# Attention scores on two row halves of the array in fp16 words, the softmax in place in PSUM, and its result turned by transfers

## The chip, the cores and the metric

The kernel runs on one core of a Trainium2 chip. The metric is device time in microseconds (us) of one execution; lower is better. PE is the TensorE matrix engine (PEld its weight loads), DVE the VectorE, ACT the ScalarE, POOL the GpSimd engine, SP the queue that issues the transfers (DMA).

## The reference, cut to what matters

Eight sequences (B) of 576 positions (S), eight heads (H) of 64 dimensions (D). Attention with a decay comes first, then a feed-forward block of 1024 channels on 4608 tokens of 512 features.

```
scores = (q @ k.T) / sqrt(D)                        # per b, h: 576 x 576
cum    = cumsum(log(clip(f, 1e-4, 1)))
scores = where(causal, -1e9, scores + cum[i] - cum[j])
attn   = exp(scores - max); attn /= sum(attn) + 1e-9
x      = attn @ v                                   # heads side by side: 4608 x 512
h      = x @ w_in                                   # 4608 x 1024
solu   = h * softmax(h)
ln     = (solu - mean) / sqrt(var + 1e-6) * g_ln
out    = ln @ w_out                                 # 4608 x 512
```

## The kernel before, in words

Two heads form a pair; there are 32 pairs, four to a sequence. A pair's 576 queries are cut into five tiles, i = 0 to 4: one of 64 rows and four of 128. Tile i meets 64 + 128 i keys, so the five tiles have 64, 192, 320, 448 and 576 columns for each head. The first three tiles are "half 0" of a pair (320 queries), the other two "half 1" (256 queries). The feed-forward block runs in 36 layers of 128 tokens; four and a half layers use one sequence.

A number that has to be exact beyond fp16 is held as two words, high and low, and a product of two such numbers is three matmuls (high by high, low by high, high by low).

- **Loading.** `load` brings a pair's q and k into `raw`; `split_qk` cuts them into a high part `hi` (POOL) and a remainder left in `raw` (`parts`, DVE or POOL), in fp32r. The remainders and copies are then laid one under the other by many small transfers into `qs`, `ks`, `kz` and `qz`, so that one matmul contracts over 128 rows: 64 rows of the one part and 64 of the other. The decay `cum` stands in two more rows of `kz`.
- **Scores.** `score_products` (lines 657, 658): for each tile and head two fp32r matmuls into one of two PSUM banks `ps`. The four pairs of the first sequence do their half 0 in plain fp32 instead (`native`, line 655), so that the first layer can start early.
- **Softmax.** `scores`: DVE adds the causal mask, scales, writes the tile to `p` in SBUF and keeps the greatest value `nm` (line 678); ACT takes the exponent in place and its sum (681); DVE makes the inverse `ri` (692, 693); POOL multiplies `p` by it (708).
- **P turned.** `transposes`: PE turns `p` in pieces of 128 by 128 against `ident` (739) into two PSUM banks `ps_t`; ACT takes out the high word `pth` (333) and DVE the low word `ptl` (747). The widest tile, i = 4, goes another way from the fifth pair on: POOL (703) and DVE (705) make its two fp16 words `p16` in SBUF, and two transposing transfers (342) turn them.
- **Values.** `values`: P turned times v into a PSUM bank `ps_o`. The first block of keys is one product over both heads (778, "whole" array); the others are one product for each head on a half of the array's columns (782). ACT and DVE take out the words `x_h` and `x_l` (801, 802).
- **Layer.** `layer`: 24 matmuls of 512 columns into `hps` (818 to 820), the softmax and the norm on DVE, ACT and POOL (831 to 864), the result turned (by transfers in layers 5 to 29, by PE otherwise) into `zz`, and 24 matmuls of 512 columns into `ps_o` (888 to 890).

What stands where in each engine's queue is not written by hand: `Plan.schedule` replays the whole program with a cost for every operation and takes, on each engine, the ready operation with the smallest due time. The due times come from the tables `DUE`, `EARLY`, `AT_P`, `AT_L` and others. PSUM banks are handed out by pools: two banks for scores (`s`), two for turning (`t`), two for outputs (`o`); `hps` holds the last two of eight. Matmuls without use (line 991) fill the gaps that the plan sees on PE in its first 140 us.

Of the kernel before, what the change touches and what calls it, by code (L numbers as in the profile page):

```python
# [24 lines left out]
HALF_S = 320  # L25
MASK = -8.0e9
# [28 lines left out]
SWITCH = ((0.0, 40.0, 0.0, 95.0), (0.0, 0.0, 0.0, 95.0), (0.0, 10.0, 0.0, 95.0), (130.0, 230.0, 180.0, 0.0))  # L55
# [11 lines left out]
class Plan:  # L67
# [31 lines left out]
    def schedule(self):  # L99
# [11 lines left out]
        for _ in self.ops:  # L111
            for e in stale:
# [78 lines left out]
DUE = dict(load=77.279, split=-5.82, upper=-59.07, v=-11.029, S=((-16.591, 2.389), (-10.866, -1.366), (-5.374, -8.943), (-5.783, 2.152), (-2.369, 2.528)), T=((-4.114,), (-6.578,), (0.027, -77.756), (12.862, 14.095), (-144.678, 29.668, 76.368)), V=((16.423, 371.464), (24.511, 165.955)))  # L191
EARLY = dict(load=-5.393, split=100.725, upper=-110.557, v=36.25, S=((216.478, -198.746), (23.491, -109.734), (23.153, -123.713), (-123.145, 60.456), (26.752, 113.365)), T=((-12.366,), (-36.759,), (-81.739, -143.07), (38.749, -11.206), (-229.138, -88.73, -36.262)), V=((-26.507, -137.733), (60.804, 84.836)))
PAIR = 23.079
C_OUT = 31.47
START = 86.666
HALF = ((64.967, -14.868), (32.745, -34.71))
W_IN = (-57.941, 54.591)
W_OUT = (103.025, 310.791)
LOAD = (198.891, -63.738)
WI_SCALE = (-43.671, -130.632)  # L200
VDUE = ((-38.21, -22.856, 38.942), (79.121, -21.859, -165.431), (55.69, -110.294, -55.795))
W_SCALE = 138.576
W_DMA = (-134.941, 217.289)
LAYER = PAIR * NPAIR / 4.5
AT_P = (-81.617, 13.065, -70.797, 41.914, 10.593, 20.603, -9.689, -6.751, -9.556, -4.733, 6.888, -145.035, -0.228, -5.232, -11.649, -239.734, 11.35, 1.454, -1.658, -3.713, -18.063, -464.917, -48.735, -17.963, -2.737, -28.57, 0.178, -5.187, -1.852, -244.035, -23.722, -77.279)
# [7 lines left out]
def tile_kernel(ctx: ExitStack, tc: tile.TileContext, qk, v, f, w_in, w_out, g_ln, out):  # L213

    nc = tc.nc  # L220
# [7 lines left out]
    plan = Plan(s=2, t=2, o=2)  # L228
# [22 lines left out]

    qz = [sb(f"qz_{c}", 2, w, dtype=F32R) for c, w in enumerate((320, 256))]
    pt = [sb("p_0", P)] + [sb(f"p_{i}", (2 * i + 1) * P) for i in range(1, NQ)]
    mask = sb("mask", S + P, dtype=BF16)

    def masks():
# [5 lines left out]
        nc.gpsimd.memset(pt[0], 0.0)  # L262
# [775 lines left out]
```

## Time and profile before

| | |
|---|---|
| time, three runs | 761.96, 762.23 (median), 763.01 us |
| span of the profiled execution | 757.0 us; 5.2 us less than the median run |
| PE busy | 722.8 us (95% of the span), 4983 matmuls, 462 of them fillers |
| DVE, ACT, POOL busy | 608.3 us (80%), 474.1 us (63%), 456.7 us (60%) |
| transfers | 133.87 MB, 75.3% of sixteen DMA engines' span |
| TensorE clock granted | 0.998 on average |

A time in the text is in us from the start of the span. A matmul's busy time includes the pipeline behind it, so two matmuls that follow each other at once overlap in such a row; what a matmul costs PE is read from the distance between starts. A row "x24" counts 24 instructions.

### The profile page before, as it was taken

How to read it: one execution, taken by the hardware profiler on the slowest of the kernel's cores; microseconds unless marked ns; L12 is line 12 of the kernel's file. 1: busy time of each engine (PE TensorE's matmuls, PEld its weight loads, DVE VectorE, ACT ScalarE, POOL GpSimd, SP SyncE). 2: the span in 40 equal slices, each digit the busy share in tenths (PEclk: the TensorE clock that was granted, in tenths of full speed). 3: DMA queues.
4: the chain of work that ended last, by engine and by line, in shares of the span. 5: the costliest groups of instructions: out<-in, count | busy, mean ns of one | idle time of the engine just before them, and what ended most of it. 6: DMA issues, size and time to landing. Idle time of an engine off the chain costs nothing. (4 is left out here: it accounts for less than half of the span.)

```text
span 757.0 us, 15810 instructions
## 1 busy us (share of the span) xinstructions
PE 722.8 (95%) x4983; PEld 453.5 (60%) x4983; DVE 608.3 (80%) x1828; ACT 474.1 (63%) x1239; POOL 456.7 (60%) x645
## 2 busy tenths in 40 slices
PE   8998999988999999999999999999999999999998
PEld 7775676655656566555556666555565555554445
DVE  6557888899997899989599999999897869883343
ACT  5698977676665667755466677655565556653333
POOL 5537496656674787668377777775786666531220
PEclk9999999999999999999999999999999999999999
DMA  9557948968879898989789899889899788442001
GB/s 320 139 210 207 272 115 223 206 169 213 197 172 214 173 239 177 225 207 213 165 188 211 200 228 213 202 206 192 189 206 202 146 192 166 95 106 42 29 15 42
DMA packets 176851, 134.87 MB, mean 178 GB/s; under 512 B 128704, under 2 KB 139712, under 8 KB 175744
## 3 DMA queue, kind: packets, MB, share of 16 engines
q1 hardware_dynamic: 176768, 133.87, 75.3%
q8 instruction: 39, 0.64, 0.4%
q14 instruction: 44, 0.36, 0.2%
HBM read 39.51 MB, written 10.03 MB: 65 GB/s over the span
## 5 line engine op out<-in xcount | busy, mean ns | idle before, releaser
L681 ACT ACTIVATE p<-p,nm 128x320 f32<-128x320 f32 (+4 forms) x320 | 177.1, 554 | 88.7 <-DVE nm L678 83.4
L708 POOL TENSOR_SCALAR p<-p,ri 128x192 f32<-128x192 f32 (+4 forms) x264 | 153.2, 594 | 90.2 <-DVE ri L693 66.2
L678 DVE CUSTOM_DVE_ANT_0 p<-ps,mask 128x320 f32<-128x320 f32 (+4 forms) x320 | 126.3, 419 | 16.0 <-PE ps L658 11.2
L657 PE MATMUL ps<-ks_f32r,qs_f32r 128*128 128x448 f32 (+4 forms) x360 | 120.6, 359 | 4.6 <-DVE nm L678 3.7
L333 ACT ACTIVATE pth_f<-ps_t 128x512 f16<-128x512 f32 (+4 forms) x200 | 85.2, 442 | 46.1 <-PE ps_t L739 41.3
L818 PE MATMUL hps<-wi_h,x_h 128*128 128x512 f16 x288 | 109.9, 381 | 0.5 <-DVE e L840 0.5
L888 PE MATMUL ps_o<-wo_f,zz 128*128 128x512 f16 x280 | 106.8, 381 | 2.6 <-DMA zz<-z 2.2
L820 PE MATMUL hps<-wi_h,x_l 128*128 128x512 f16 x288 | 109.1, 379 | 0.0
L819 PE MATMUL hps<-wi_l,x_h 128*128 128x512 f16 x288 | 109.1, 379 | 0.0
L890 PE MATMUL ps_o<-wo_f,zz 128*128 128x512 f16 x280 | 106.1, 379 | 0.4 <-DVE zz L880 0.4
L889 PE MATMUL ps_o<-wo_f,zz 128*128 128x512 f16 x280 | 106.1, 379 | 0.0
L739 PE MATMUL ps_t<-ident,p 128*128 128x128 f32 x548 | 90.8, 279 | 13.1 <-DVE ptl_f L747 4.6
L658 PE MATMUL ps<-kz_f32r,qz 128*128 128x448 f32 (+4 forms) x360 | 100.8, 296 | 2.0 <-DMA kz_f32r<-c_scratch 1.2
L747 DVE TENSOR_TENSOR ptl_f<-ps_t,pth_f 128x512 f16<-128x512 f32 (+3 forms) x188 | 91.9, 502 | 8.1 <-ACT pth_f L333 7.7
L739 PEld LDWEIGHTS ps_t<-ident,p 128*128 128x128 f32 x548 | 64.4, 141 | 45.6 <-POOL p L708 13.0
L657 PEld LDWEIGHTS ps<-ks_f32r,qs_f32r 128*128 128x128 f32 (+1 forms) x360 | 64.9, 182 | 23.9 <-DVE nm L678 11.8
L589 POOL TENSOR_SCALAR hi<-raw 128x576 fp32r<-128x576 f32 (+1 forms) x64 | 48.4, 756 | 35.4 <-DMA kz_f32r<-raw 13.1
L658 PEld LDWEIGHTS ps<-kz_f32r,qz 128*128 128x128 f32 (+1 forms) x360 | 65.2, 182 | 5.1 <-issue 1.5
L850 POOL TENSOR_SCALAR st<-st 128x1 f32<-128x1 f32 x36 | 11.1, 308 | 89.0 <-ACT z L846 79.2
L703 POOL TENSOR_SCALAR wo_p<-p,ri 128x576 f16<-128x576 f32 x56 | 47.1, 851 | 27.9 <-DVE ri L693 14.8
L831 DVE TENSOR_REDUCE st<-hps 128x1 f32<-128x1024 f32 x36 | 43.9, 1218 | 21.1 <-PE hps L820 20.8
L681 ACT ACTIVATION_READ_ACCUMULATOR p<-p,nm 128x1 f32 (+1 forms) x320 | 60.1, 188 | 0.0
(194 smaller groups left out, 1416.2 us busy)
## 6 DMA issues: line engine op xcount, KB each, us to landing
raw<-in_qk_dram SPq DMA_DIRECT2D x32, 576.0 KB
ks_f32r<-hi SPq DMA_DIRECT2D x128, 144.0 KB
kz_f32r<-raw SPq DMA_DIRECT2D x64, 144.0 KB
vraw<-in_v_dram SPq DMA_DIRECT2D x28, 320.0 KB
out_dram<-y SPq DMA_DIRECT2D x35, 256.0 KB
qs_f32r<-hi SPq DMA_DIRECT2D x56, 144.0 KB
qs_f32r<-raw SPq DMA_DIRECT2D x56, 144.0 KB
qz<-hi SPq DMA_DIRECT2D x56, 80.0 KB
```

Of the source, the lines that this page charges most:

```text
L657: nc.tensor.matmul(dst, qs(p)[:, h, q0:q0 + nq], ks(p)[:, h, cols], start=True, stop=False)
L658: nc.tensor.matmul(dst, z[:, h, z0:z0 + nq], kz(p)[:, h, cols], start=False, stop=True)
L678: op(DVE, R_NS[i], at + 0.5, lambda a=a, e=e, key=key, o0=o0: nc.vector.tensor_tensor_reduce(pr[:, a:e], ps[plan.place[key]][:nq, o0:o0 + ...
L681: op(ACT, E_NS[i], at + 1.3, lambda: nc.scalar.activation(pr, pr, AF.Exp, bias=x, scale=-1.0, accum_out=sm[m][i][:nq, h:h + 1]), [("nm", m ...
L708: op(POOL, N_NS[j], at + 2.8, lambda g=g, j=j, pg=pg, r1=r1: nc.gpsimd.tensor_scalar(pg, pg, r1, 1.0, ALU.mult, ALU.mult), [("ri", m, j)], ...
L739: nc.tensor.transpose(tp[:, s, :], pt[i][:, k * P:(k + 1) * P], ident)
L818: nc.tensor.matmul(hps[:, sl], x_h, wi_h[:, c, sl], start=(c == 0), stop=False)
L819: nc.tensor.matmul(hps[:, sl], x_h, wi_l[:, c, sl], start=False, stop=False)
L820: nc.tensor.matmul(hps[:, sl], x_l, wi_h[:, c, sl], start=False, stop=(c == NCC - 1))
L888: nc.tensor.matmul(o, zz[a][:, 0, j], wo(0, k), start=(k == 0), stop=False)
L889: nc.tensor.matmul(o, zz[a][:, 0, j], wo(1, k), start=False, stop=False)
L890: nc.tensor.matmul(o, zz[a][:, 1, j], wo(0, k), start=False, stop=(k == NFC - 1))
```

## The change

Most of the attention is written anew, with new tables for the order. The layer's arithmetic stays.

- **q and k** become fp16 words, high and low, on the 64 rows of their own head: the two heads of a pair stand on rows 0 to 63 and 64 to 127 of one tile `qk16` and nothing is moved by transfers. So that fp16 holds them, q, k and v are scaled by powers of two per sequence: ACT sums their squares (`squares`, line 486) and `scale` works out three factors where it worked out one. High words are made on POOL (`Q_HI`), low words on DVE (567). The decay rows are now three bf16 words in `crow`.
- **Scores.** For a tile, each head has four matmuls on its half of the array's rows: three of words (606) and one that adds the decay rows (604); the two heads' matmuls alternate. Each head has a bank of its own. The plain fp32 start is gone.
- **Softmax in place.** Tiles 0 to 3 stay in their PSUM bank (`HOME`): mask, exponent, and both words of P are made from there, the high word on ACT (333), the low word on DVE (658). Tile 4 still goes through SBUF (`p_4`) and POOL. The bank comes free after the low word.
- **P turned** by transfers alone, for all tiles and pairs, both words in one transfer per tile.
- **Values** go tile by tile of queries: products of 64 or 128 columns (680, 683) where they had 128 to 320.
- **PSUM**: one pool of six banks, each a tile of its own, for scores, outputs and turning.
- **Layer**: `e`, `z` and `y` have two buffers; z is turned by transfers in layers 3 to 32, its high word is made by ACT and its low word by POOL (it was POOL and DVE). The last sequence's two halves are planned apart.

```
-P_32, X_32 = (1, 1, 2, 1), (1, 2, 2, 1, 1, 2, 1, 2)
-TURN = (450.0, 15.0, 1700.0)
+TURN = (1100.0, 22.0, 1700.0, 6.0)
-TURNED = (5, 30)
-Z_ENG = (3, 3, 1, 2)
+TURNED = (3, 33)
+Z_ENG = (3, 1)
+Z_LO = (3,) * 36
+Q_HI = (3,) * 32
+P_HI = (1, 1, 1, 1, 3)
+HOME = (1, 1, 1, 1, 0)
...
-    plan = Plan(s=2, t=2, o=2)
+    plan = Plan(s=NS)
...
-    ps = [pp.tile([P, 512], F32, name=f"ps{n}") for n in range(2)]
+    ps = [pp.tile([P, 512], F32, name=f"ps{n}") for n in range(NS)]
     hps = pp.tile([P, DFF], F32, name="hps")
-    ps_t = [pp.tile([P, 4, P], F32, name=f"ps_t{n}") for n in range(2)]
-    ps_o = [pp.tile([P, 512], F32, name=f"ps_o{n}") for n in range(2)]
...
-                    nc.tensor.matmul(dst, qs(p)[:, h, q0:q0 + nq], ks(p)[:, h, cols], start=True, stop=False)
-                    nc.tensor.matmul(dst, z[:, h, z0:z0 + nq], kz(p)[:, h, cols], start=False, stop=True)
+                for n, (x, y) in enumerate(((hi, hi), (lo, hi), (hi, lo), (None, None))):
+                    for h in range(2):
+                        k0 = P * (4 - i) if h == 0 else 0
+                        dst, cols = bank(p, i, h, int(a > 0))[:, :e - a], slice(k0 + a, k0 + e)
+                        if x is None:
+                            nc.tensor.matmul(dst, pattern[row(h)], crow[row(h), (p // NPAIR) % 2, p % NPAIR, cols], start=False, stop=True)
+                        else:
+                            nc.tensor.matmul(dst, x[row(h), 0, q0:q0 + P], y[row(h), 1, cols], start=(n == 0), stop=False)
...
+        def home(i, h, nq=P):
+            w = 64 + P * i
+            return bank(p, i, h)[:nq, :w] if HOME[i] else pt[i][:nq, h * w:(h + 1) * w]
...
-                op(POOL, N_NS[j], at + 2.8, lambda g=g, j=j, pg=pg, r1=r1: nc.gpsimd.tensor_scalar(
-                    pg, pg, r1, 1.0, ALU.mult, ALU.mult), [("ri", m, j)], [("p", j, g)])
+            copied(P_HI[j], {POOL: N_NS[j], ACT: 158 + 0.83 * w, DVE: 67 + 1.05 * w}, at[j][g] + STEPS[3], h16, lambda j=j, g=g, nq=nq: home(j, g, nq),
+                   reads, [("p16", n2, j, g)], scale=r1, clear=prior, port=not HOME[j])
...
-                nc.tensor.transpose(tp[:, s, :], pt[i][:, k * P:(k + 1) * P], ident)
+        turned_dma(at, lambda: turned_p(p, i).rearrange("p x s w -> p (x s) w"), lambda: p16(p, i)[:nq], nq // 16 * 2 * (2 * i + 1),
+                   [(x, m, i, h) for x in ("p16", "p16l") for h in range(2)], [("pt", m * (i < 3), i)], clear=to)
...
+            for j in range(i + 1):
+                for c, (x, y) in enumerate(((0, 0), (1, 0), (0, 1))):
+                    if j == 0:
+                        nc.tensor.matmul(o[:, a:a + n], v16[m][:, x, :2].rearrange("p t d -> p (t d)"), t[:, y, i], start=(c == 0), stop=(i == 0 and c == 2))
+                        continue
+                    for h in range(2):
+                        nc.tensor.matmul(o[row(h), a:a + n], v16[m][:, x, 2 * j + h], t[:, y, i + j if h else i - j], start=False, stop=(j == i and c == 2))
```

Three places show what becomes of the order. First PE, in the middle of the run, where values are multiplied. Before, the row halves do not exist and a whole product has 256 columns; a pair's scores stand between its whole products and its column halves (`ps_o1` is the output's bank, `pth_1` and `ptl_1` the words of P turned, `v16_0` those of v):

```order
L778 LDWEIGHTS v16_0_78
L778 MATMUL ps_o1_153<-pth_1_f16_979,v16_0_78 128x256
L778 LDWEIGHTS v16_0_78
L778 MATMUL ps_o1_153<-ptl_1_f16_985,v16_0_78 128x256
L657 MATMUL ps0_147<-ks_1_f32r_903,qs_1_f32r_856 128x288
L658 MATMUL ps0_147<-kz_1_f32r_851,qz_1_64 128x288
L657 MATMUL ps1_148<-ks_1_f32r_903,qs_1_f32r_856 128x288
L658 MATMUL ps1_148<-kz_1_f32r_851,qz_1_64 128x288
L782 LDWEIGHTS v16_0_78
L782 MATMUL ps_o1_153<-pth_1_f16_979,v16_0_78 64x256
```

After, the first query tile of half 1 ends a run of column halves (`t0_1_p` is P turned of half 0, `t1_0_p` that of half 1) and the next opens with three whole products, which are followed by halves again:

```order
L683 MATMUL ps2_146<-t0_1_p_739,v16_3_81 64x128
L680 LDWEIGHTS v16_2_80
L680 MATMUL ps0_144<-t1_0_p_1502,v16_2_80 128x128
L680 LDWEIGHTS v16_2_80
L680 MATMUL ps0_144<-t1_0_p_1502,v16_2_80 128x128
L680 LDWEIGHTS v16_2_80
L680 MATMUL ps0_144<-t1_0_p_1502,v16_2_80 128x128
L683 LDWEIGHTS v16_2_80
L683 MATMUL ps0_144<-t1_0_p_1502,v16_2_80 64x128
```

What moved: the array changes between whole, row halves and column halves more often. Over the whole program PE passes from one of these forms to another 430 times after the change, 128 times before; it has 480 whole and 1920 half products of values where it had 180 and 1104.

The second place is PE's scores, after the change: the two heads' matmuls alternate, each head with its own bank (`ps3` and `ps4`), the decay rows last (before, the four rows of lines 657 and 658 above are a tile's scores):

```order
L606 MATMUL ps3_147<-qk16_3_72 128x448
L606 LDWEIGHTS qk16_3_72
L606 MATMUL ps4_148<-qk16_3_72 128x448
L604 LDWEIGHTS pattern_74
L604 MATMUL ps3_147<-crow_73,pattern_74 128x448
L604 LDWEIGHTS pattern_74
```

What moved: four matmuls and four weight loads for each head and tile, where there were two.

The third place is the queue of transfers, SP, in mid-run. Before, the two transposing transfers of the widest tile stand among the small transfers that lay out q and k:

```order
L342 DMA_TRANSPOSE pth_1_f16_979<-wo_1_p16_2109 128x9x128
L342 DMA_TRANSPOSE ptl_1_f16_985<-wo_1_p16_2109 128x9x128
L339 DMA qs_1_f32r_856<-hi_0_73 64x576
L339 DMA qz_0_63<-hi_0_73 64x320
L339 DMA qs_1_f32r_856<-raw_1_72 64x576
L339 DMA qs_1_f32r_856<-hi_0_73 64x576
L339 DMA qz_0_63<-hi_0_73 64x320
```

After, nearly all that is left are transposing transfers (`128x18x128` is eighteen squares of 128 by 128) of P and of z:

```order
L342 DMA_TRANSPOSE t1_0_p_1502<-wo_0_p16_1480 128x18x128
L342 DMA_TRANSPOSE zz16_0_105<-z_0_103 128x16x128
L342 DMA_TRANSPOSE t0_1_p_739<-p16s_1_83 128x10x128
L342 DMA_TRANSPOSE t0_1_p_739<-p16s_1_83 128x6x128
L342 DMA_TRANSPOSE t0_1_p_739<-p16s_1_83 128x2x64
L339 DMA crow_73<-c_scratch 3x4x576 x2
L342 DMA_TRANSPOSE zz16_1_106<-z_1_104 128x16x128
L339 DMA raw_3_68<-in_qk_dram 128x1152
```

What moved: the copies of q and k inside SBUF are gone, and transposing transfers carry 2.3 times as many elements: 16,384 blocks of 16 by 128 fp16 elements where there were 7,232. SP issues 287 instructions for 598.

More of the change, by code (lines that the diff above doesn't have):

```diff
@@ L193 @@
[L193 to L205, printed above, removed]
@@ new lines, in tile_kernel, with rows @@
+    raw = [sb(f"raw_{n}", 2, S) for n in range(NRAW)]
+    qk16 = [sb(f"qk16_{n}", 2, 2, S, dtype=F16) for n in range(NQK)]
+    crow = sb("crow", 2, NPAIR, S, dtype=BF16)
+    pattern = sb("pattern", P, dtype=BF16)
+    def rows():
+        nc.gpsimd.memset(pattern, 0.0)
+        for r in (0, D):
+            nc.gpsimd.memset(pattern[r:r + 3], -8.0 * QK)
+    op(POOL, 500, -64, rows, writes=[("pattern",)])
+    for n in range(2):
+        op(DVE, 900, -64 + 60 * n, lambda n=n: nc.vector.memset(crow[:, n], 0.0), writes=[("crow0", n)])
@@ new lines, in scale @@
+        op(DVE, 700 if e < 3 else 1050, due, exponents, [key], sk)
+        op(PE, 150, due, lambda: nc.tensor.matmul(ps_t(key)[:, 3, :2 * m].rearrange("p (c j) -> p c j", j=m), ones, v[:1], start=True, stop=True), [*sk, ("ones",)], [key], dense=False)
+        def factors():
+            got = ps_t(key)[:, 3, :2 * m].rearrange("p (c j) -> p c j", j=m)
+            if a == 0:
+                nc.vector.tensor_scalar(v[:, 0, :1], got[:, 0, :1], 2.0 ** (-24 if x == "wo" else -14), None, ALU.mult)
+            nc.vector.tensor_scalar(v[:, 1], got[:, 1], 2.0 ** 13, None, ALU.mult)
@@ L800, in values @@
+        for i in tiles:
+            ns = 3 * (q_n(i) * SHORT + 3) + 6 * i * 30
+            op(PE, ns, at + 0.2 * (i - tiles[0]), lambda i=i: product(i), [("pt", p % 2 * (i < 3), i), ("v16", m), ("v16l", m)], [key],
+               take=key if i == tiles[0] else None, clear=[xk], form=HALVES if i else WHOLE)
+        up = 1.0 / P_UP
         xo = [t[:, hp, x0:x0 + w] for t in x16]
-        op(ACT, 160 + 0.9 * w, at + 1.5, lambda: nc.scalar.activation(xo[0], ps_o[plan.place[key]][:, :w], AF.Copy, scale=up), rk, [xk])
@@ L885, in product_out @@
+            op(ACT, 500, at + 0.5, lambda a=a, key=key: nc.scalar.copy(zz[:, a, 0], ps_t(key)), [key], zk[:1])
+            op(DVE, 683, at + 1.0, lambda a=a, key=key: nc.vector.tensor_tensor(
+                zz[:, a, 1], ps_t(key), zz[:, a, 0], ALU.subtract), [key, zk[0]], zk[1:])
+        at += 1.0 + at_out
+        key, yt, yk = ("s", "o", "y", n), yts[n % 2], ("y", n % 2)
         def product_out(k):
[L886 removed]
+            o = ps[plan.place[key]]
             a, j = divmod(k, 4)
[L888 removed]
@@ L979, in tile_kernel @@
         layers((p + 1) // NPAIR * S)
+    for half in range(2):
+        for n in range(NPAIR):
+            p = (B - 1) * NPAIR + n
+            at = FINAL[half][0] + FINAL[half][1] * n
+            if half == 0:
+                if n == 0:
+                    prepare_batch(B - 1, at)
+                whole(p, at, LATE)
+            half_of(p, half, at, LATE)
+        layers((B - 1) * S + (320, S)[half])
     blank = ident.bitcast(BF16)
```

736 lines of the change are left out of this document (313 added, 423 removed).

## The prediction

> **What bounds the kernel now.** The page's first two parts come first: which engine is full, and where.
>
> ```profile
> PE 722.8 (95%) x4983; PEld 453.5 (60%) x4983; DVE 608.3 (80%) x1828; ACT 474.1 (63%) x1239; POOL 456.7 (60%) x645
> PE   8998999988999999999999999999999999999998
> DMA  9557948968879898989789899889899788442001
> ```
>
> PE is full nearly everywhere. The view by stretches then divides the span into a start, a steady part and an end of layers alone; its later rows (674 on) are used for the transfers.
>
> ```profile
> 0.00:205.00 205.00, 189.12 (x1438) 136.08 (x1438) 162.16 (x510) 150.23 (x386) 124.45 (x197) 0.99 0.76 207
> 205.00:655.00 450.00, 436.86 (x2984) 265.12 (x2983) 396.77 (x1200) 281.96 (x769) 309.62 (x415) 1.00 0.88 195
> 690.00:757.00 67.00, 62.85 (x337) 33.28 (x335) 24.57 (x49) 23.86 (x41) 10.39 (x17) 1.00 0.08 28
> 674.00:690.00 16.00, 15.02 (x106) 7.66 (x103) 8.43 (x15) 5.33 (x10) 2.48 (x3) 1.00 0.53 87
> 690.00:695.00 5.00, 5.00 (x28) 2.77 (x27) 0.00 (x0) 1.20 (x3) 1.93 (x3) 1.00 0.14 52
> 10.00:20.00 10.00, 10.00 (x95) 8.95 (x93) 5.75 (x7) 5.85 (x10) 3.78 (x8) 1.00 1.02 391
> ```
>
> From 205 to 655 us PE is busy 97% of the time, DVE 88% (396.77 of 450), the transfers 88%: PE sets the pace, two others are close. The groups of that stretch say how much work it holds.
>
> ```profile
> L739 PE MATMUL ps_t<-ident,p 128*128 128x128 f32 x346 | 57.7, 277 | 5.4 <-DVE ptl_f L747 2.8 <-POOL p L708 1.2 <-POOL st L851 0.9
> L747 DVE TENSOR_TENSOR ptl_f<-ps_t,pth_f 128x512 f16<-128x512 f32 (+3 forms) x132 | 63.4, 494 | 7.1 <-ACT pth_f L333 6.8
> L333 ACT ACTIVATE pth_f<-ps_t 128x512 f16<-128x512 f32 (+3 forms) x132 | 55.8, 438 | 30.7 <-PE ps_t L739 26.3 <-issue 1.7 <-DVE ptl_f L747 0.4
> L705 DVE SCALAR_TENSOR_TENSOR wo_p<-p,ri,wo_p 128x576 f16<-128x576 f32 x44 | 40.4, 944 | 0.8 <-POOL wo_p L703 0.8
> L802 DVE SCALAR_TENSOR_TENSOR x_l<-ps_o,x_h 128x256 f16<-128x256 f32 (+1 forms) x45 | 20.0, 447 | 1.2 <-ACT x_h L801 0.9
> L860 DVE TENSOR_TENSOR z<-e,z 128x1024 f16<-128x1024 f32 x23 | 30.9, 1342 | 4.2 <-POOL z L335 4.2
> L592 DVE TENSOR_TENSOR raw<-raw,hi 128x576 fp32r<-128x576 f32 x22 | 20.3, 922 | 1.0 <-POOL hi L589 0.6 <-issue 0.3
> L692 DVE TENSOR_SCALAR ri<-sm 128x2 f32<-128x2 f32 (+1 forms) x88 | 27.6, 313 | 11.8 <-ACT p L681 11.7
> L681 ACT ACTIVATE p<-p,nm 128x448 f32<-128x448 f32 (+4 forms) x220 | 121.8, 554 | 68.6 <-DVE nm L678 64.1 <-POOL v L627 2.0 <-POOL p L708 0.6
> L681 ACT ACTIVATION_READ_ACCUMULATOR p<-p,nm 128x1 f32 (+1 forms) x219 | 41.1, 188 | 0.0
> L678 DVE CUSTOM_DVE_ANT_0 p<-ps,mask 128x320 f32<-128x320 f32 (+4 forms) x219 | 86.3, 419 | 5.5 <-PE ps L658 5.1
> L831 DVE TENSOR_REDUCE st<-hps 128x1 f32<-128x1024 f32 x24 | 29.2, 1218 | 4.5 <-PE hps L820 4.3
> ```
>
> 24 layers (L831) and 22 pairs (L705 comes twice a pair). Last the order of time on PE, where starts give what a matmul costs: a piece mid-run, three rows of the chain (start, time, what), and three rows of the first 206 us.
>
> ```profile
> 647.04 0.49 PE L739 MATMUL ps_t<-ident,p 128*128 128x128 f32 x3
> 647.37 0.38 PE L778 MATMUL ps_o<-pth_f,v 128*128 128x256 f16 x2
> 647.59 0.27 PE L778 MATMUL ps_o<-ptl_f,v 128*128 128x256 f16 x1
> 647.79 0.41 PE L782 MATMUL ps_o<-pth_f,v 128*64 128x256 f16 x4
> ...
> 648.47 0.28 PE L782 MATMUL ps_o<-pth_f,v 128*64 128x128 f16 x4
> 648.58 0.22 PE L782 MATMUL ps_o<-ptl_f,v 128*64 128x128 f16 x2
> 648.64 0.38 PE L782 MATMUL ps_o<-pth_f,v 128*64 128x256 f16 x4
> ...
> 649.06 0.40 PE L657 MATMUL ps<-ks_f32r,qs_f32r 128*128 128x288 f32 x1
> ...
> 649.71 0.39 PE L888 MATMUL ps_o<-wo_f,zz 128*128 128x512 f16 x1
> ```
> ```profile
> 402.65 0.57 PE ps_o L778 x3
> 404.70 0.61 PE ps_o L782 x12
> 410.47 0.22 PE hps L820
> ```
> ```profile
> 3.41 17.07 PE L991 MATMUL hps<-ident 128*128 128x256 bf16 x143 [3.41 <-POOL ident masks.py:199]
> ...
> 34.38 0.49 PE L774 MATMUL ps_o<-pth_f,vraw 64*64 64x320 f32 x2
> ...
> 205.68 0.39 PE L818 MATMUL hps<-wi_h,x_h 128*128 128x512 f16 x1
> ```
>
> **The change, part by part,** over the steady stretch, in PE's time.
>
> *P turned.* 346 turns go. Three take 0.33 us (647.04 to 647.37), so 0.11 each: -38.1.
>
> *Scores.* Today four matmuls of 288 columns take 0.65 us (649.06 to 649.71), 0.564 ns a column; a pair has 4 x 1600 columns: 3.61 us, 79.4 for 22 pairs. After, two heads run side by side: 4 terms x 1600 columns at 0.22/512 = 0.43 ns make 2.75 us, 60.5. No row has two matmuls on row halves with all 128 columns. If they do not overlap it is 5.5 us, 121. The nearest row is 34.38: two matmuls on opposite quarters, one on either row half, are both done 0.49 us after the first began, so they overlapped. I take 60.5: -19 (the other end +42).
>
> *Values.* Today 1.69 us for half 1 (647.37 to 649.06) and 0.57 + 0.61 for half 0: 2.87 a pair, 63.1. After, 60 column halves of at most 128 columns: six take 0.17 (648.47 to 648.64), 0.028 each, 1.70. Fifteen whole products of at most 128 columns: those of 256 take 0.11, so between 0.055 and 0.11; I take 0.08, 1.2. Each change of the array's form costs 0.09 (the step 647.59 to 647.79 is 0.20 where its neighbours are 0.11); a pair has 430/32 = 13.4 where it has 4 now, row halves taken at the same price: 1.2. Sum 4.1, 90: +27 (ends +19 and +36).
>
> The Trainium skill ("TensorE: Matmul & The Clock Gate", LDWEIGHTS) prices a weight load by its columns, 107 ns for 128, whatever the rows. By it the narrowest two tiles of scores would cost four loads on each half, 0.43 us instead of 0.11 and 0.33, and the scores' term would be -10; but the trace's six half products with a load each in 0.17 us show that loads overlap, and I keep -19.
>
> Sum on PE: -38 - 19 + 27 = -30, if today's 13 us of idle time and the shorter waits stay.
>
> *The other engines must let PE have it.* DVE loses L747 (63.4), gains low words for four tiles (1024 columns for each head in four instructions; L802's 447 ns is for some 285 columns, so about 1.5 us a head, 66), the second remainder (+20, L592), loses z's (-30.9) and, where the sum's home is PSUM, perhaps half of L692 (-14): 375 of 420, as full as today. ACT trades L333 (55.8) for the high words (about as much) and gains 44 squares of 576 columns and 24 high words of z of 1024; at L681's 554 ns for some 320 columns these are 1.0 and 1.8 us, 87: at most 370 of 420, 88%. POOL loses L708 and half of L592's kind and gets lighter. None passes PE; what the fuller ACT makes wait is the bank that it reads, below.
>
> *Transfers.* The transposing ones can be weighed where they are nearly alone; the queue's rows there:
>
> ```profile
> 675.65 1.30 SPq L342 DMA_TRANSPOSE pth_f<-wo_p  x1
> 677.04 0.53 SPq L339 DMA_DIRECT2D out_dram<-y  x1
> 678.04 1.28 SPq L342 DMA_TRANSPOSE ptl_f<-wo_p  x1
> 679.99 2.61 SPq L342 DMA_TRANSPOSE zz<-z  x2
> ```
>
> From 674 to 690 us these are two of 72 and two of 64 blocks and one output; 0.53 x 16 = 8.5 us of the sixteen engines, less the output's 0.14 x 5 = 0.7, over 272 blocks: 28.6 ns a block. The stretch would then need (22 x 392 + 24 x 128) x 28.6 = 334 us; raw q and k, v and outputs are 26.5 MB, 69 us at the 391/1.02 GB/s of 10 to 20 us. 403 in all, against 0.88 x 450 = 396 today: of 420 us, 96%. This becomes the second bound. SP itself spends 1.3 us on a transposing transfer and has 160 + 30 of them, under 300 us even at 1.5; but its queue is in order, and one that waits for a low word holds loads and outputs behind it. Those are due a sequence ahead, so I price that at nothing.
>
> The Trainium skill ("DMA: Bandwidth & Descriptors", Latency and other measured facts) gives 261 GB/s for a transposing transfer, 16 ns for a block of 4096 bytes, which would make 184 + 69 us and no bound at all; the row's 28.6 is dearer, and it decides.
>
> *Start and end.* All 740 fillers of the new order stand before the third layer (462 stand before the fourth now): at 17.07/143 = 0.119 us each, +33 us of PE time, laid where PE waits for others; the plain fp32 work goes. Up to the sixth layer I count 116 us of products at the prices above, 88 of fillers and the first 3.4 of waiting: 207, against 205.7 now, of which 16 are idle (189.12 busy). If none of that idle time is inside the fillers it is +16, if all of it, about 0; no row divides it, and I take +7. The end (690 to 757) is PE's 24 products a layer, which stay: 0.
>
> Span: 757.0 - 30 + 7 = 734; with the 5.2 us between the span and the median run, **739 us**. Its own range, from the ends of values and start: 722 to 755.
>
> **The rivals.**
> *Banks (slower).* Six banks for everything. A tile kept in place holds its bank through mask, exponent, inverse and two word-makings. Today's pace is 450/22 = 20.5 us a pair, 123 bank-us. The widest tile's four banks (some 2.5 us each), two outputs and a layer's bank take about 22; six banks of tiles 0 to 3 may then be held (123 - 22)/6 = 16.8 us each before the pace falls under today's. Bare, the hold is two heads of 0.42 (L678), 0.55 + 0.19 (L681), 0.44 (L333) and 0.49 (L747), 0.31 and more for the inverse (L692) and the product's 0.7: about 5.5 us. DVE and ACT are visited five times, and at 88% busy a visit may wait behind another group's work, 1 us each by the length of the rows above: I expect 8 to 12. At 18 us a pair would take 21.7, +26: 795. The Trainium skill ("TensorEngine Tiling (Array Packing)", PSUM Pressure) says that row tiles must write different banks, which is why no bank can be saved. Chance 0.16.
> *Transfers set the pace (slower).* If the rest of the traffic moves not at 383 but at today's mean of 195/0.88 GB/s, it takes 120 us and the stretch 454/0.98 = 463: +13, 782. It decides from a rest of about 110 us. For it: the digits of 9 in the DMA line; against: today's small rows are what goes. Chance 0.12.
> *Row halves do not overlap* (the change would not do what it says): -38 + 42 + 27 + 7, 800. The row at 34.38 speaks against it. Chance 0.07.
> *PE's waits shrink too (faster than forecast).* fp32r loads and two score banks go; if 10 us of idle and as much of short waits vanish, 715. Chance 0.13.
>
> **How the numbers follow.** The forecast has 0.48; another 0.04 is left for a gain that the start eats up. 0.2% (1.5 us) is about what a measurement of this kernel can tell from nothing. Faster: 0.48 + 0.13 + 0.03 from the upper edge of the transfers' case = 0.64; same 0.05; slower 0.31. The range 706 to 788 takes in the forecast, most of the quicker case, the transfers' case and half of the banks'.
>
> **What would show it.** Right: P's turns gone from PE; two score matmuls a few ns apart; 128-column halves 0.03 us apart; PE still over 90% busy mid-run; a mid-run layer in about 17.5 us instead of 18.75. Wrong: score groups on PE waiting for DVE's low word (658); value products waiting for the transfers; a DMA share of 0.98 in the steady stretch; the sixth layer later than 220 us; or, the other way, PE idle yet the whole shorter because the forms change for less than 0.09.

## The result, and the profile after

The changed kernel takes 772.1 us (median of four runs, 768.2 to 774.8) where the kernel before takes 762.6 in the runs beside it: a ratio of 1.0113, 95% interval 1.0065 to 1.0162. It is 1.1% slower where 3% faster was forecast. In the profiled executions the span went from 757.0 to 766.4 us.

The page's first two parts of the changed kernel:

```profile
PE 704.3 (92%) x6524; PEld 397.5 (52%) x6524; DVE 629.9 (82%) x1935; ACT 556.7 (73%) x1435; POOL 298.8 (39%) x343
PE   8999989988687988999999979899999999999998
PEclk9999999989699999999999989999999999999999
```

TensorE is still the fullest engine, with 18 us less busy time than before; VectorE gained 22 us, ScalarE 83, GpSimd lost 158. The line of the granted clock dips to 8 and 6 tenths between 153 and 211 us; the last section comes back to it.

The sixth layer's product starts at 233.1 us after the change and the thirtieth's at 663.2; before they start at 205.7 and 655.5. Cut there, the view by stretches reads as follows (columns: length; busy time and count of PE, weight loads, DVE, ACT, POOL; granted clock; DMA share; GB/s), first the kernel before, then the changed one, then the fillers alone in the start of each (L991 before, L904 after).

```profile
0.00:205.70 205.70, 189.82 (x1445) 136.77 (x1446) 162.86 (x513) 150.86 (x387) 125.06 (x198) 0.99 0.76 207
205.70:655.50 449.80, 436.66 (x2979) 264.62 (x2978) 396.51 (x1202) 281.82 (x770) 309.50 (x414) 1.00 0.88 194
655.50:757.00 101.50, 96.30 (x563) 52.14 (x561) 48.91 (x117) 41.45 (x84) 22.13 (x35) 1.00 0.20 47
```
```profile
0.00:233.10 233.10, 206.31 (x2092) 141.72 (x2093) 193.45 (x584) 176.34 (x458) 76.32 (x103) 0.95 0.70 175
233.10:663.20 430.10, 398.04 (x3730) 204.43 (x3729) 383.39 (x1218) 332.70 (x889) 189.39 (x206) 0.99 0.77 153
663.20:766.40 103.20, 99.99 (x707) 51.31 (x703) 53.03 (x135) 47.66 (x89) 33.07 (x34) 1.00 0.48 93
```
```profile
0.00:205.70 205.70, 56.49 (x462) 45.42 (x462) 0.99 0.76 207
```
```profile
0.00:233.10 233.10, 88.77 (x740) 72.01 (x740) 0.95 0.70 175
```

The difference of 9.4 us is +27.4 in the start, -19.7 in the middle, +1.7 at the end. Not all of the 19.7 is a gain: counted by products, the middle now holds the scores of 20.7 pairs (744 of L606, 36 a pair) where it held 21.9 (263 of L657, 12 a pair), and the end one more. Read TensorE's column without the fillers: 722.8 - 56.5 = 666.3 us before (the total of the three stretches), 704.3 - 88.8 = 615.5 after. **TensorE's work fell by 51 us, close to the forecast (30 in the middle and, from 133 to 116, 17 in the start); none of it arrived.** The fillers took 32 of it, and idle time, in which no product runs, the rest and 9 more: 34.2 us of the span without a product before, 62.1 after (15.9 to 26.8 in the start, 13.1 to 32.1 in the middle).

What ended TensorE's longest waits in the middle (233 to 663 us) of the changed kernel (waiting line, releaser: us, times, longest; 22.3 of the 32.1 us):

```profile
PE ps L680 <- DVE p16s L658: 5.2, 4, 2.7
PE hps L712 <- DVE e L734: 4.4, 4, 1.9
PE ps L472 <- DVE scale L470: 3.5, 4, 1.5
PE ps L606 <- DVE x_l L692: 3.3, 6, 1.3
PE ps L606 <- DVE wo_p L658: 3.0, 3, 2.4
PE ps L680 <- DMA t_p<-wo_p: 2.9, 2, 2.5
```

Five of the six end with a VectorE instruction, but at many places and never for long: no single wait makes up the idle time.

### The profile page after: what moved, and what is told of

It is laid out like the page before. It is cut to its first block, busy times and chain, and to the rows that moved or that the text cites. A ratio compares the mean times of both kernels' runs of the same rounds, so it can differ in the third digit from the quotient of the medians.

```text
span 766.4 us, 18006 instructions
## 1 busy us (share of the span) xinstructions
PE 704.3 (92%) x6524; PEld 397.5 (52%) x6524; DVE 629.9 (82%) x1935; ACT 556.7 (73%) x1435; POOL 298.8 (39%) x343
## 4 chain that ended last, share of the span: by engine, by line
PE 24%; DVE 19%; ACT 5%; issue 3%; DMA 1%; POOL 1%; DVEq 0%; ACTq 0%; POOLq 0%
PE ps L781 3%; PE ps L783 3%; PE ps L782 3%; DVE ps L626 3%; DVE wo_p L658 3%; PE hps L712 3%; PE ps L683 2%; PE hps L714 2%; PE hps L713 2%; DVE p16s L658 2%; PE ps L606 2%; DVE p L626 2%; DVE st L725 2%; DVE e L734 2%; DVE qk L567 2%
## 5 line engine op out<-in xcount | busy, mean ns | idle before, releaser
L631 ACT ACTIVATE ps<-ps,nm 128x320 f32<-128x320 f32 (+3 forms) x256 | 113.6, 444 | 27.7 <-DVE nm L626 25.0
L606 PE MATMUL ps<-qk 64*128 64x288 f16 (+4 forms) x1152 | 101.7, 284 | 20.2 <-DVE p16s L658 8.1
L781 PE MATMUL ps<-wo_f,zz 128*128 128x512 f16 x280 | 106.6, 381 | 6.2 <-DVE zz L773 1.8
L626 DVE CUSTOM_DVE_ANT_0 ps<-ps,mask 128x192 f32<-128x192 f32 (+3 forms) x256 | 103.7, 442 | 8.0 <-PE ps L604 6.3
L782 PE MATMUL ps<-wo_f,zz 128*128 128x512 f16 x280 | 106.1, 379 | 0.0
L783 PE MATMUL ps<-wo_f,zz 128*128 128x512 f16 x280 | 106.1, 379 | 0.0
L753 POOL TENSOR_TENSOR z<-e,z 128x1024 f16<-128x1024 f32 x30 | 68.0, 2266 | 51.6 <-ACT z L333 50.5
L333 ACT ACTIVATE p16s<-ps,ri 128x320 f16<-128x320 f32 (+2 forms) x192 | 69.5, 413 | 16.7 <-DVE ri L643 10.5
L606 PEld LDWEIGHTS <-qk 64*128 64x128 f16 x1152 | 47.6, 96 | 63.9 <-issue 39.6
L904 PEld LDWEIGHTS <-ident 128*128 128x128 bf16 x740 | 72.0, 100 | 16.2 <-issue 3.3
L658 DVE SCALAR_TENSOR_TENSOR p16s<-ps,ri,p16s 128x320 f16<-128x320 f32 (+2 forms) x192 | 72.5, 407 | 8.5 <-ACT p16s L333 6.2
L683 PE MATMUL ps<-t_p,v 128*64 128x128 f16 x1920 | 79.3, 224 | 0.0
L904 PE MATMUL hps<-ident 128*128 128x256 bf16 x569 | 68.0, 280 | 1.4 <-POOL ident masks.py:199 1.4
L739 ACT ACTIVATE junk<-e,st 128x1024 bf16<-128x1024 f32 x36 | 41.3, 1147 | 30.5 <-DVE st L735 27.1
```

What stands on the lines that cost most here:

```text
L606: nc.tensor.matmul(dst, x[row(h), 0, q0:q0 + P], y[row(h), 1, cols], start=(n == 0), stop=False)
L626: op(DVE, R_NS[i] if n == 0 else 442, at[i][h] + STEPS[0], lambda i=i, h=h, n=n, a=a, e=e, x=x, m0=m0: nc.vector.tensor_tensor_reduce(home ...
L631: op(ACT, E_NS[i], at[i][h] + STEPS[1], lambda i=i, h=h, x=x: nc.scalar.activation(home(i, h), home(i, h), AF.Exp, bias=x, scale=-1.0, acc ...
L658: op(DVE, L_NS[j], at[j][g] + STEPS[4], lambda j=j, g=g, nq=nq, h16=h16, l16=l16, r1=r1: nc.vector.scalar_tensor_tensor(l16(), home(j, g, ...
L683: nc.tensor.matmul(o[row(h), a:a + n], v16[m][:, x, 2 * j + h], t[:, y, i + j if h else i - j], start=False, stop=(j == i and c == 2))
L781: nc.tensor.matmul(o, zz[:, a, 0, j], wo(0, k), start=(k == 0), stop=False)
```

## The experiments

Except for two that say so, the order of every engine's instructions was kept as in the changed kernel (or the kernel before), and only the named instructions were left out, moved or repeated. Theory V says that VectorE sets the pace, P that TensorE does, W that no one engine does. Gains are in us of the kernel before, by the difference of the ratios; the changed kernel's own ratio carries +-0.5%, 4 us.

**What sets the pace: fillers, TensorE, VectorE.**

*No fillers.* `if ... share(t)` became `if ... share(t) and t > 140.0e3` where the fillers are issued.

> The changed kernel without its 740 filler products of the start (L904, 86 us of TensorE); the order of all else is kept. Theory V (VectorE's queue sets the start): the fillers lie in holes that TensorE has anyway, the sixth layer stays at 233 us give or take 4, the time at 768 to 778 (a lower clock in the start may cost a few us). Rival F (the fillers stand in TensorE's way, 33 us more of them than before the change): the sixth layer at 200 to 215, the time 740 to 755.

Measured 776.1 us, ratio 1.0184 [1.0158, 1.0210]: 5 us longer, the sixth layer at 232.9:

```profile
0.00:232.90 232.90, 141.62 (x1352) 78.50 (x1353) 193.84 (x584) 176.44 (x458) 76.16 (x103) 0.84 0.68 175
```

Without the fillers' 88.8 us TensorE is busy 141.6 us of the start for 206.3 (the other products take longer, at a granted clock of 0.84 for 0.95), and the start is as long: the fillers lie in holes. F falls.

*No decay products.*

```
-  nc.tensor.matmul(dst, pattern[row(h)], crow[...], start=False, stop=True)
```

> The changed kernel without the 384 decay products (L604; the decay is left out of the scores), order kept: TensorE loses 36 us of work over the program and a fourth of its score products. Theory V: TensorE is waiting already, so the time falls by 0 to 8 us (764 to 772), its idle time grows by the rest. Rival P (TensorE still sets the pace of the middle): 23 us leave the middle, 737 to 750.

Measured 773.1, ratio 1.0144 [1.0107, 1.0182]: nothing gained, 1 us above V's range. P falls for the changed kernel.

*Low words of q and k on GpSimd.*

```
-  nc.vector.scalar_tensor_tensor(x16_[1], x, s, x16_[0], ALU.mult, ALU.subtract)
+  nc.gpsimd.tensor_scalar(x, x, s, 1.0, ALU.mult, ALU.mult); nc.gpsimd.tensor_tensor(x16_[1], x, x16_[0], ALU.subtract)
```

> The low words of q and k (L567, 64 of 0.83 us, 53 us of VectorE) are made by GpSimd in two instructions at the same place of the order; GpSimd goes from 299 to some 430 us. Theory V: the time falls by a third to two thirds of the 53 us, 735 to 755, with the sixth layer before 222. Rival B (the six score banks set the pace, for reasons other than VectorE): 765 to 775. Rival P: 765 to 775.

Measured 793.1, ratio 1.0409 [1.0372, 1.0446]: all expectations missed, it is 23 us longer. Its page's first part, the moved line (count: shortest/median/longest ns, first and last start), and the longest of GpSimd's waits, here and in the changed kernel:

```profile
PE 711.2 (90%) x6524; PEld 399.3 (51%) x6524; DVE 601.5 (76%) x1871; ACT 556.6 (71%) x1435; POOL 422.9 (54%) x471
```
```profile
L567 POOL TENSOR_SCALAR raw<-raw,scale x64: 737/745/1323, 22.4 to 645.3; 128x576 f32<-128x576 f32 x64
L567 POOL TENSOR_TENSOR qk<-raw,qk x64: 1272/1277/1902, 23.2 to 646.1; 128x576 f16<-128x576 f32 x64
```
```profile
POOL st L743 <- ACT junk L739: 92.6, 21, 12.2
```
```profile
POOL st L743 <- ACT junk L739: 100.6, 25, 12.1
```

The words take 2.0 us instead of 0.8, and now stand in a queue that waits 93 us for ScalarE's squares of the layers. That wait is not new, the words behind it are. So the move does not test VectorE's load alone; which of the two, the longer words or the queue, costs the 23 us is not shown.

*The low words twice.* The same line, `for _ in range(2)`.

> The same low words (L567) made twice on VectorE: 53 us more of VectorE, 683 in all, nothing else changed. Theory V: 25 to 50 us longer, 797 to 822. Rivals B and P: 772 to 785.

Measured 834.2, ratio 1.0955 [1.0918, 1.0992]: 64 us longer for 66 us more of VectorE (695.7 busy). V was near (12 us above its range), and everything else far off; taken alone it would have been read as proof that VectorE is the bound. The next run shows that it is not.

*No low words.* L567 left out, the low halves zeroed once.

> The low words of q and k are not made (L567 left out; the low halves of the buffers are zeroed once): 53 us less of VectorE, the order of everything else kept. Theory V (VectorE's queue sets the pace of start and middle): 30 to 55 us shorter than the changed kernel, 717 to 742, since doubling them cost 62. Rival L (it is the way of a pair from split to scores that counts, not VectorE's load: the low word lies ahead of the first score): the gain stays under 15 us, 757 to 772.

Measured 763.2, ratio 1.0000 [0.9976, 1.0023]: 9 us shorter for 42 us less of VectorE (587.8 busy). V, which asked for 30 to 55, falls in that form, and rival L's range holds the result: **work added to VectorE cost its full time, work taken away gave back a fifth.**

*Squares twice.* L486, `for _ in range(2 if j else 1)`.

> The squares of q and k (L486, 64 of 0.68 us and 0.19 for the read) are made twice: 55 us more of ScalarE, 612 in all, order kept. They too lie ahead of the scores, a sequence earlier. Theory V: ScalarE has room (73% busy), 3 to 18 us longer, 775 to 790. Rival C (VectorE and ScalarE hand each tile to one another, and either one's load counts alike): 40 to 60 us longer, 812 to 832.

Measured 799.9, ratio 1.0488 [1.0446, 1.0530]: 29 us longer for 47 us more of ScalarE (603.4 busy), which is "only" 73% busy. Between the two theories: a fuller ScalarE costs as well, 0.6 us for each us added.

**Two that were planned anew.** In these the planner ordered everything again.

> As in the run with the low words on GpSimd, but the planner knows the engine and its 2.03 us, and orders everything anew. If that run was slow because GpSimd's queue held the low words behind waits that were not planned, the time falls under the changed kernel's, 745 to 765, by 53 us less of VectorE. If it was slow because GpSimd and VectorE slow one another (VectorE lost only 28 us of busy time there), 770 to 795.

> The first sequence's q and k get a fixed scale of 4 instead of one from squares and a scale chain (left out for this sequence), planned anew: the first scores start near 28 us instead of 44.9. Theory N (the first scores wait for the first scales, and this is what the start lost with the plain fp32 scores): the first layer starts at 66 to 74 instead of 83.9 and the end moves with it, 755 to 765. Theory V alone: VectorE has idle time in the first 84 us only (22 us), so the fifth and sixth layer move by 5 to 12 and the time is 760 to 768. Rival K (later pieces bind, the start has slack): sixth layer at 230 to 236, 768 to 776.

Measured 818.6 (1.0726 [1.0680, 1.0772]) and 832.9 (1.0921 [1.0874, 1.0967]), far outside every expectation: 47 and 62 us longer than the changed kernel, and the first 24 longer than the same words on GpSimd in the old order. The likely reason, not tested, is that the due times in the tables fit one plan. A new plan under old tables lost more here than any edit won, so neither run says anything about its edit, and the runs after these kept the order.

**Transfers, TensorE and VectorE together, and the kernel before.**

*Two buffers for turned tiles 3 and 4* (`t{half}_{p % 2}`), on top of the kernel without decay products (and without the transfers of their rows).

> The changed kernel without the decay products (as in the run that left them out, which makes the room in SBUF; 773 us) and with two buffers instead of one for the turned P of tiles 3 and 4; order kept. Theory T (the transfers that turn P wait for the one buffer, SP's in-order queue waits with them, and this is what binds now): 10 to 30 us under 773, 743 to 763. Rival W (no one resource binds; orders and hand-overs of all engines do): 768 to 775.

Measured 773.7, ratio 1.0136 [1.0081, 1.0190]; without the second buffer it was 773.1. The buffer does not bind.

*Half of P turned:* `turned_p(p, i)[:, 0]` from `p16(p, i, 0)`.

> Only the high word of P is turned by transfers (the low word's half of each turned tile is zeroed once, so the low words do not reach the output): 8192 of the 16384 transposing blocks of P go, some 200 us of the sixteen transfer engines' 550, order and count of all instructions kept. Theory T: 15 to 40 us shorter, 732 to 757. Rival W: up to 8 us shorter, 764 to 772.

Measured 767.2, ratio 1.0064 [1.0039, 1.0090]: 4 us, which the two intervals do not tell from nothing. (The expectation counted z's blocks with P's: P has 32 x 392 = 12,544 of the 16,384, and 6272 of them went.) The queue's row of the changed kernel (span 766.4) and of this run (765.1):

```profile
q1 hardware_dynamic: 284150, 115.14, 70.2%
```
```profile
q1 hardware_dynamic: 183798, 89.45, 51.1%
```

That is 538 and 391 us of the sixteen engines: 147 us went, 23 ns a block, and 4 came back. Theory T falls.

*Neither decay products nor low words of q and k.*

> Neither decay products nor low words of q and k: TensorE 36 us and VectorE 53 us lighter at once, order kept; alone they gave -0 and -9. If TensorE and VectorE take turns as the bound: 20 to 45 us shorter than the changed kernel, 727 to 752. If neither binds (transfers, banks or hand-overs do): 756 to 765, the sum of the two.

Measured 763.8, ratio 1.0009 [0.9978, 1.0039]: the gain of the low words alone. TensorE's 36 us are worth nothing even beside a lighter VectorE.

*The kernel before with one score product.*

```
-  nc.tensor.matmul(dst, qs..., ks..., start=True, stop=False)
-  nc.tensor.matmul(dst, z..., kz..., start=False, stop=True)
+  nc.tensor.matmul(dst, qs..., ks..., start=True, stop=True)
```

> The kernel before with one score product instead of two (L658, 350 products, 53 us of TensorE, left out), order kept: the counterpart of leaving out the decay products. If TensorE sets the pace of the kernel before, as the prediction read it: 25 to 45 us shorter, 717 to 737. If it does not: 752 to 762.

Measured 758.6, ratio 0.9945 [0.9913, 0.9977]: 4 us. The middle of that run (sixth to thirtieth layer), to be laid beside the second row of the kernel before above:

```profile
204.40:655.30 450.90, 413.21 (x2718) 231.38 (x2718) 397.82 (x1203) 280.24 (x769) 309.86 (x414) 1.00 0.89 194
```

TensorE's busy time fell from 436.7 to 413.2 and the middle takes 450.9 us for 449.8. TensorE's idle time there rose from 13.1 to 37.7 us. The engine that was 97% busy there did not set the pace.

**Words of P, the first scales, and all at once.**

*Low words of P left out from the third pair on*, for tiles 0 to 3 (`p > 1 and j < 4 or nc.vector...`) and for tile 4 (`j == 4`).

> The low words of P are not made for tiles 0 to 3 from the third pair on (240 of L658, 109 us of VectorE; the low halves keep the first two pairs' words), order kept; each score bank is free one VectorE visit sooner. If VectorE's work on the way (L658 and L626 lead the chain of waits of the changed kernel) sets the pace: 25 to 45 us shorter, 727 to 747, and about twice what leaving out tile 4's low words gives. Banks bind besides: more than three times that run's gain. No one resource (theory W): 757 to 768.

> The same for tile 4 alone, whose scores lie in SBUF (60 of L658, 58 us of VectorE); no bank is freed sooner. If VectorE's work on the way sets the pace: 10 to 25 us shorter, 747 to 762. Theory W: 764 to 770.

Measured 754.1 (0.9900 [0.9869, 0.9931]) and 759.8 (0.9972 [0.9950, 0.9994]): 16 us for 87 of VectorE (543.4 busy), and 11 for 49 (581.3 busy), again a fifth. The first lies between the ranges of the two theories, the second inside VectorE's and below W's: VectorE's work on the way counts, but for a fifth. The edit that also frees score banks sooner gains no more for each us than the one that does not: the banks add nothing that these runs can tell.

*The fixed scale with the order kept*, no fillers.

> The fixed scale of 4 for the first sequence's q and k with the order kept, and without the fillers (which would hold TensorE until 45 us); to be compared with the run without fillers (776, first layer 78.1, sixth 232.9). Theory N (the wait of the first scores for the first scales is what the start lost): first scores near 30, first layer 64 to 72, sixth layer 220 to 226, 764 to 770. Rival K (the later pairs of the start bind): sixth layer 230 to 233, 772 to 778.

Measured 769.4 (1.0101 [1.0073, 1.0129]), 6 us under the run without fillers; first layer 75.1, sixth 230.4. Theory N has the sign and a part of the size: the time is in N's range, the first layer later than its 64 to 72, the sixth in K's range. The first scores moved only from 39.3 to 35.2 us, because the weights' scale (L472) stands ahead of them in TensorE's queue:

```profile
34.70 0.58 PE L472 MATMUL ps<-scale,ones 1*128 1x2 f32 x2 [5.95 <-DVE scale L463]
35.22 0.34 PE L606 MATMUL ps<-qk 64*128 64x64 f16 x6
```

L472 itself waits 5.95 us for VectorE.

*The kernel before without low words of the turned P* from the third sequence on (`p >= 2 * NPAIR or nc.vector...`).

> The kernel before without the low words of the turned P (L747) from the third sequence on, 144 of some 0.49 us, 70 us of VectorE, order kept. Leaving out 53 us of TensorE gave 4. If VectorE set the pace of the kernel before already: 20 to 45 us shorter, 717 to 742. Theory W (there, too, no one resource): 752 to 762.

Measured 755.1, ratio 0.9922 [0.9894, 0.9950]: 6 us for 45 of VectorE (563.3 busy). VectorE did not set the pace of the kernel before either.

*All of it at once* (no low words of q and k, none of P from the third pair, no decay), *and few squares* (L486 over 8 columns).

> All that was taken from VectorE and TensorE one by one, at once: no low words of q and k, no low words of P from the third pair on, no decay products: VectorE 220 us lighter, TensorE 36, order kept. One by one they gave 9 + 18 + 12 + 0 = 39 us. Theory W (no one resource; the order's hand-overs): not more than that sum, 730 to 745. If VectorE hid TensorE's saving: 45 to 75, 697 to 727. If ScalarE or the score banks bind as soon as VectorE is lighter: less than the sum, 745 to 755.

> The squares of q and k (L486, 64 of 0.68 us) over 8 of the 576 columns: some 30 us of ScalarE less, order kept (the scales come out larger). Theory W: 3 to 8 us shorter, 764 to 769, as VectorE's words gave a fifth of their time. If ScalarE sets the pace of the start (no relief of TensorE, fillers or VectorE moved the fifth layer by more than 3 us there): the sixth layer at 216 to 226 instead of 233 and 752 to 762.

Measured 733.2 (0.9618 [0.9598, 0.9638]) and 768.7 (1.0087 [1.0051, 1.0124]). The first is 38 us under the changed kernel, the sum of the single gains (9 + 16 + 11 + 0 = 36): theory W, neither the surplus of a hidden TensorE nor the shortfall of a next bound. The page's row shows where VectorE went:

```profile
PE 681.2 (93%) x6140; PEld 379.3 (52%) x6140; DVE 443.7 (61%) x1571; ACT 552.6 (76%) x1435; POOL 282.5 (39%) x347
```

VectorE has 186 us less to do, and a fifth of it returned once more. The second gives 2 us for 28 of ScalarE, which its interval does not tell from nothing, and its sixth layer starts at 231.7: a lighter ScalarE does not shorten the start.

No kernel that makes all the words came out under the kernel before.

**Where the returned part can be read.** The page's part 4 of each kernel shows the chain of waits that ended last. It was followed back to 380 us before and to 359 after, so its shares, which add up to about half the span, hold for the later half alone. First the kernel before.

```profile
PE 26%; DVE 16%; DMA 3%; issue 2%; POOL 1%; ACT 1%; SPq 0%; DVEq 0%; POOLq 0%; ACTq 0%
DVE p L678 3%; PE ps_o L888 3%; PE ps_o L890 3%; PE ps_o L889 3%; PE hps L818 3%; PE hps L820 3%; PE hps L819 3%; DVE wo_p L705 2%; DVE ptl_f L747 2%; DMA zz<-z 2%; PE ps_t L739 2%; PE ps_o L782 2%; DVE z L860 2%; PE ps L657 2%; PE ps L658 1%
```
```profile
PE 24%; DVE 19%; ACT 5%; issue 3%; DMA 1%; POOL 1%; DVEq 0%; ACTq 0%; POOLq 0%
PE ps L781 3%; PE ps L783 3%; PE ps L782 3%; DVE ps L626 3%; DVE wo_p L658 3%; PE hps L712 3%; PE ps L683 2%; PE hps L714 2%; PE hps L713 2%; DVE p16s L658 2%; PE ps L606 2%; DVE p L626 2%; DVE st L725 2%; DVE e L734 2%; DVE qk L567 2%
```

| left out | engine's busy time fell by | on the chain, later half | gained, whole run |
|---|---|---|---|
| before: L658, second score product | 32 | 1%, 8 us | 4 |
| before: L747, low words of turned P | 45 | 2%, 15 us | 6 |
| after: L604, decay | 12 | not listed | 0 |
| after: L567, low words of q and k | 42 | 2%, 15 us | 9 |
| after: L658, low words of P | 135 | 3% + 2%, 38 us | 27 |
| after: half of P's turning | 147 of the transfer engines | DMA 1% (all transfers), 8 us | 4 |

Across engines, what a line was worth goes with the chain rather than with busy time: the transfers' 147 us and TensorE's 32 returned 4 each, VectorE's 42 returned 9. Within VectorE the two say the same. The chain is no price list: its percents are whole, every line returned less than its share (0.4 to 0.7 of it), and the share covers half the run. (TensorE's busy time is modelled and falls by less than the count of products: the two score edits took out an estimated 53 and 36 us by the distance of starts.)

## Why the prediction was wrong, step by step

**What bounds the kernel now: this step failed.** It read the busy columns, 97% of TensorE in the middle, and concluded that TensorE sets the pace. Leaving out 53 us of its products returned 4 (kernel before) and 36 returned 0 (after); leaving out all fillers did not shorten the start. The chain was on the same page: of its 49% it gave TensorE half and VectorE a third, and of the P turns that were to bring -38 it lists 2% (L739), 15 us of the later half. The prediction took three of the chain's rows for prices of a product and left its shares unread.

Of the 33 us between 739 and 772, 20 lie in the start (+27 for +7), 10 in the middle (-20 for -30), 2 at the end.

**The terms on TensorE were right.** The turns of P are gone. Row halves overlap:

```profile
150.41 0.57 PE L606 MATMUL ps<-qk 64*128 64x320 f16 x6
150.82 0.30 PE L604 MATMUL ps<-crow,pattern 64*128 64x320 bf16 x2
151.05 0.39 PE L712 MATMUL hps<-wi_h,x_h 128*128 128x512 f16 x1
```
```profile
161.92 0.86 PE L683 MATMUL ps<-t_p,v 128*64 128x128 f16 x24
162.71 0.26 PE L680 MATMUL ps<-t_p,v 128*128 128x64 f16 x3
```

Eight score products of 320 columns take 0.64 us: 0.16 for two, 0.50 ns a column where 0.43 was taken and 0.86 would mean no overlap. 24 half products take 0.79, 0.033 each (0.028 taken). In the middle TensorE's busy time fell by 38.6, with about a pair less in that stretch; -30 was forecast. (The values' price uses the 13.4 changes of form a pair, which the trace bears out: 430. Before it shows 184 and not 128, as the narrowest score tiles use half the columns too; the sum does not use that number.)

**"If today's 13 us of idle time and the shorter waits stay"** was the condition under the sum, and it broke: 13.1 became 32.1. The sum stood on the one engine whose work was worth almost nothing. Most signs that were to show the forecast right came all the same: P's turns gone, half products 0.033 us apart, TensorE 93% busy in the middle, a middle layer in 17.9 us for 18.7. Only the sixth layer, later than 220 us, and 5 us of waits of score products for the low word (658) in the middle spoke against it.

**The other engines.** Sizes held: VectorE 383 of 430 us (375 of 420 forecast), ScalarE 333 (at most 370), transfers 0.77 of the middle (0.96 forecast at 28.6 ns a block, where the half-turned run shows 23; and not a bound: half of the turning returned 4 us; the trace counts 295 transfers for 718). "None passes PE" does not follow from shares under 100%: ScalarE at 73% and VectorE at 82% each lengthened the program at once when they got more to do. The change gave VectorE 22 us and ScalarE 83.

**The start: +7 forecast, +27 measured, the term most mis-sized.** It failed by the same step. The forecast added up TensorE's work (116 us of products, 88 of fillers, 3.4 of waiting: 207) and took the start to be little longer, 213. The work was right (117.5 and 88.8); the waiting was 26.8, and the start 233.1. The fillers cost the first layer 6 us (83.9, without them 78.1) and the sixth none. The other products shrank from 133.3 to 117.5 us, and that did not shorten the start. What the prediction passed over in half a sentence ("the plain fp32 work goes") is what the first scores now wait for:

```profile
44.88 0.26 PE L606 MATMUL ps<-qk 64*128 64x64 f16 x6
45.01 0.41 PE L606 MATMUL ps<-qk 64*128 64x192 f16 x6
```
```profile
20.32 0.70 PE L655 MATMUL ps<-kz_k,qs_q 65*128 65x320 f32 x2
```

The scores of the first sequence began without a scale before; after, squares, scale and words come first, 24.6 us later (19.0 without fillers, 39.34), and the first layer starts at 83.9 for 71.6. Fixing those scales returned 6 us with the order kept. (The narrowest tile's eight products took 0.13 us, 44.88 to 45.01; 0.11 was taken. A weight load of L606 takes 96 ns on average, so the loads overlap.)

So 12 of the 27 us are there at the first layer and 14 at the fourth (169.7 for 156.1); the fifth is 29 late (216.5 for 187.5). Between the fourth and the fifth the new order has the scores of 2.5 pairs where the old one had 1.8, and there lies the longest wait of the start for a score bank, 4.0 us:

```profile
PE ps L606 <- DVE p16s L658: 5.8, 3, 4.0
```

No run changes that stretch alone. The rest of the start's 27 is not settled: fillers, TensorE, low words and squares, each relieved by itself, moved the sixth layer by 4 us at most, all of VectorE's and TensorE's together by 9.

**The end** was 1.7 for 0.

**The rivals.** Banks: by the trace a bank of tiles 0 to 3 was held 8.6 us on average in the middle, from the first score product of its tile to the end of its low word, 16.5 at most; 8 to 12 were expected and 16.8 needed before banks set the pace. Half of the transfers' turning returned 4 us, and the row halves overlap. "PE's waits shrink too" came out the other way (and its own terms, 739 less 10 and 10, give 719 and not 715). The result lies in the range, but there by luck, since the rival that happened was not among them: that the kernel before was no longer held by TensorE, so that what a lighter TensorE saves is lost and what VectorE and ScalarE get more is paid.

**What stays open.** That TensorE did not set the pace is shown. That no one engine does (W) is what is left when each fails: GpSimd was not relieved by itself, and ScalarE only by 28 us. Why the balance is +9 and not -5 or +20 is argued, not shown: by the prices of the runs 22 us more of VectorE cost 4 to 21, 83 more of ScalarE cost anything up to 51, and TensorE's 51 return 0 to 6. And the new order is a rival that no run tests: the two new plans lost 24 us against the same edit in the old order and 62 against the changed kernel, so a part of the 9 may lie in the tables.

## What to carry to other kernels

In a kernel like this one, whose order is fixed and whose engines wait for one another everywhere, do not book removed busy time as gained time: here it returned from nothing to a fifth, while added time cost 0.6 to 1.0 of itself (two runs). Look at a line's share on the chain of waits first; it is rough, but here it was never exceeded. The busiest engine is not thereby the bound, and one run that leaves out some of its work tells it. Doubling a cost made VectorE look like the bound here, and leaving the same cost out showed that it is not; do both. Change costs without a new plan, or a new order under old tables (here 47 and 62 us) drowns the edit.

## What was not expected of the hardware

Twice in the start after the change TensorE's granted clock fell to half after a stretch in which it was thinly used:

```profile
160.00:164.00 4.00, 1.86 (x34) 1.26 (x33) 3.79 (x15) 2.44 (x8) 0.00 (x0) 1.00 0.77 148
164.00:168.00 4.00, 3.08 (x23) 2.01 (x23) 3.83 (x14) 1.57 (x4) 1.34 (x4) 0.51 0.87 239
192.00:196.00 4.00, 0.96 (x21) 0.70 (x21) 3.83 (x15) 3.84 (x14) 1.47 (x2) 0.85 0.30 68
196.00:200.00 4.00, 1.41 (x8) 0.44 (x8) 3.77 (x14) 3.38 (x11) 2.32 (x4) 0.50 0.67 131
```
```profile
169.65 0.61 PE L712 MATMUL hps<-wi_h,x_h 128*128 128x512 f16 x1
170.05 0.63 PE L713 MATMUL hps<-wi_l,x_h 128*128 128x512 f16 x1
170.48 0.59 PE L714 MATMUL hps<-wi_h,x_l 128*128 128x512 f16 x1
```

After 1.86 busy us in four the clock is at 0.51, and after 0.96 at 0.50; 512 columns then take 0.40 to 0.43 us instead of the 0.22 of full speed. Yet without any filler the whole start ran at a mean of 0.84 and the sixth layer came no later (232.9): there a slower TensorE was time that it would have waited. The 5 us which that run lost fall in the middle (438 us for 430, at 0.97 for 0.99).

GpSimd's instructions cost VectorE time of its own: with the low words moved to GpSimd VectorE's busy time fell by 28.4 us (629.9 to 601.5), with the same words left out by 42.1 (to 587.8). The difference of 14 us is other VectorE rows that took longer; the low words of tile 4, which are read from SBUF, went from 60.1 to 65.7 us.
